# Zero matmuls in fp32, and another place for W1-W2, the transposes and the values, in a block-sorted attention with a two-way maximum layer

## The chip, the cores and the metric

The kernel runs on one core of a Trainium2 chip. The metric is the device time of one execution in microseconds (us). A core has five engines with a queue of instructions each: PE (TensorE, matmuls and transposes into PSUM; its weight loads are shown apart as PEld), DVE (VectorE), ACT (ScalarE), POOL (GpSimd, which here issues nearly all loads) and SP (SyncE, which issues the stores). An engine takes its instructions in the order of the program and stops at one whose operands are not ready. Line numbers are those of the kernel before (L77), unless a row is said to be of the changed kernel, whose lines lie a few numbers further on.

## What is computed

For 4 batches of 8 heads, 768 positions and 64 values per head, an 8 x 8 matrix `P` per head is normalised five times along rows and columns. With it the 8 blocks of 96 positions of `k` and `v` are mixed. Each block of `q` then attends to its mixed block alone. The result, 3072 tokens of 512 values, goes through a layer that takes the larger of two products.

```python
for _ in range(5):
    P = np.exp(P - np.max(P, axis=-1, keepdims=True))
    P = P / (np.sum(P, axis=-1, keepdims=True) + 1e-09)
    P = P / (np.sum(P, axis=-2, keepdims=True) + 1e-09)
k_sorted = np.einsum('bhij,bhjcd->bhicd', P, k_b)
v_sorted = np.einsum('bhij,bhjcd->bhicd', P, v_b)
scores = scale * np.matmul(q_b, k_sb.transpose(0, 1, 2, 4, 3))
attn = np.exp(scores - np.max(scores, axis=-1, keepdims=True))
attn = attn / (np.sum(attn, axis=-1, keepdims=True) + 1e-09)
x = np.matmul(attn, v_sb)          # then 3072 tokens x 512
g = np.maximum(x @ w1, x @ w2)
out = g @ w_out                    # 3072 x 512
```

## The kernel before

The maximum is rewritten: max(x W1, x W2) = relu(x (W1-W2)) + x W2. So the kernel makes W1-W2 in place of W1 (`w_difference(t)`, a quarter of the columns each, on DVE, L456), the product Wc = W2 W_out (`w2_transposes` on PE, L424, copied to `w2T`; `w_product`, L445), and then out = relu(x (W1-W2)) W_out + x Wc. A unit `moe_h(b, ch, t)` (L472) makes two of the eight 128-row blocks of the hidden layer for half a batch's tokens, 8 matmuls of 384 columns; it needs the whole of xT for that half, and quarter t of W1-W2. Its relu goes to ACT (L482) or DVE (L484) into `g`. A unit `moe_out` (L500, L508) makes 128 tokens of the output.

Attention of a batch is in eight parts u. `scores(b, u)` (L345, 8 matmuls) is followed by the exponential on ACT (L353, `e`); `values(b, u)` (L370, 8 matmuls) by a reciprocal and a product on DVE (L381, L383, `x`); `x_transposes(b, t)` (L400) turns the x of parts 2t and 2t+1 and a copy on ACT or DVE puts them into xT. Parts 0 to 3 (transposes 0 and 1) belong to the first half of the batch's tokens, units h 0 to 3; the others to units h 4 to 7. In this text scores 3, values 4, W1-W2 2 and so on have these numbers, from 0.

Ahead of the attention, k and v of two batches are mixed by block-diagonal matrices: `block_diagonals` makes them from P (L230 and four steps on DVE), `sort_v(0, t)` (L322) and `sort_k(0, t)` (L305) apply them, eight and six times. sort_k takes 64 small matmuls per two t, and each two t use one third of k_raw, which is loaded in three chunks. The second half, batches 2 and 3, is prepared later in the same way, and its `block_diagonals(1)`, L230, is the first work on PE after unit h 7 of batch 0.

The order on each engine is written out by hand (`manual_schedule`): the calls in the kernel's body are the order. Before the loop over batches they are listed one by one. In the loop a batch is a list of `units`, and `tail[n]` holds what stands right behind unit n. Only the engine of some copies is found by a rule (`pick`, with a running load of ACT and DVE). PSUM is a pool of four buffers used in turn: the fifth user of the pool waits until what the first wrote is read.

`keep_streaming(ps, n)` issues n matmuls with an all-zero tile `fill` into a buffer that is written afterwards anyway. Their result is used nowhere. They stand ahead of L230 (33), sort_v 0 (16), sort_k 2 and 4 (3 and 4), scores 0 (3) and values 0 (2).

POOL issues the loads in this order: v (6), q of batch 0, k (6), the columns of W2 and W1 in turn (8), W_out (2), q of batch 1, then v and k of the second half (`load_rest`) and the last two q. All loads convert fp32 to bf16.

Of the kernel before, what the change touches and what calls it, by code (L numbers as in the profile page):

```python
# [10 lines left out]
FP32 = mybir.dt.float32  # L11
BF16 = mybir.dt.bfloat16
# [3 lines left out]
def kernel(  # L16
# [17 lines left out]
    nc = tc.nc  # L34
# [4 lines left out]
    B, H, S, D = q.shape  # L39
# [11 lines left out]
    TCH = S // 2  # L51
# [3 lines left out]
    const = ctx.enter_context(tc.tile_pool(name="const", bufs=1))  # L55
# [12 lines left out]
    def ps_bf16(name):  # L68
        return psum.tile([128, 2048], BF16, tag="ps", name=name)

    fill = const.tile([128, 512], BF16, tag="fill", name="fill")
    nc.vector.memset(fill, 0.0)  # L72

    def keep_streaming(ps, n):

        for _ in range(n):
            nc.tensor.matmul(ps[:, 0:512], fill[:, 0:128], fill, start=True, stop=True)  # L77


    load = {"A": 0.0, "D": 0.0}  # L80
# [237 lines left out]
    def sort_v(sb, t, n=0):  # L318
        ps = ps_f32("v_ps")
        keep_streaming(ps, n)  # L320
        for d in range(8):
            nc.tensor.matmul(  # L322
                ps[:, d * 128 : (d + 1) * 128],
                v_dc[:, (t * 8 + d) * BLK : (t * 8 + d) * BLK + 128],
                bd_v[sb],
                start=True,
                stop=True,
            )
# [60 lines left out]
        load["D"] += 900  # L389
        x_tiles[b, u] = x  # L390

    def x_transposes(b, t):

        ih, hh = divmod(t, 2)
        ps = ps_bf16("tx_ps")
        for n in range(2):
            x = x_tiles.pop((b, t * 2 + n))
            for ii in range(4):
                m = n * 4 + ii
                nc.tensor.matmul(  # L400
                    ps[:, m * BLK : (m + 1) * BLK],
                    x[:, ii].rearrange("p t d -> p (t d)"),
                    ident[0:BLK, 0:BLK],
                    is_transpose=True,
                    start=True,
                    stop=True,
                )
        evac(
            xT[:, b, ih, hh * 2 : hh * 2 + 2, :].rearrange(
                "p h (i c r) -> p (h i) c r", r=R, c=PB  # L410
            ),
            ps[:, 0 : 2 * TCH].rearrange("p (m r c) -> p m c r", r=R, c=PB),
            2 * TCH,
        )
# [5 lines left out]
    def w2_transposes(t):  # L420
        ps = ps_bf16("tw_ps")
        for n in range(16):
            fb, dmt = t * 4 + n // 4, n % 4
            nc.tensor.matmul(  # L424
                ps[:, n * 128 : (n + 1) * 128],
                w2_sb[:, dmt, fb * 128 : (fb + 1) * 128],
                ident,
                is_transpose=True,
                start=True,
                stop=True,  # L430
            )
        evac(
            w2T[:, t * 4 : t * 4 + 4, :].rearrange("p f d -> p (f d)"),
            ps,
            2048,
            two_x=True,
            eng="D",
        )

    def w_product(t):  # L440
# [23 lines left out]

    g_tiles = {}

    def moe_h(b, ch, t):
        ps = ps_f32("h_ps")
        for m in range(2):
            fb = t * 2 + m  # L470
            for hp in range(HP):
                nc.tensor.matmul(  # L472
                    ps[:, m * 512 : m * 512 + TCH],
                    w1_sb[:, hp, fb * 128 : (fb + 1) * 128],
                    xT[:, b, ch, hp, :],
                    start=(hp == 0),
                    stop=(hp == HP - 1),
                )
        g = gpool.tile([128, 2, TCH], BF16, tag="g", name="g")
        src = ps.rearrange("p (t f) -> p t f", t=2)[:, :, 0:TCH]  # L480
        if pick((200 + 2 * TCH) / 1.2, (130 + 2 * TCH) / 0.96) == "A":
# [59 lines left out]
    sinkhorn(4)  # L541
    turn_v("A", 8, 24)
    turn_v("D", 24, 32)
    block_diagonals(0, 33)
    turn_v("A", 32, 46)
    turn_v("D", 46, 64)
    turn_v("D", 64, 84)
    turn_v("A", 84, 96)
    for t in range(8):
        sort_v(0, t, 16 if t == 0 else 0)  # L550
        if t in (3, 5):
            q_transposes(0, (t - 3) // 2)
    for t in range(6):
        sort_k(0, t, {2: 3, 4: 4}.get(t, 0))

    SC, VA, TR = att(0)
    scores(0, 0, 3)
    SC[1]()
    SC[2]()
    values(0, 0, 2)  # L560
    SC[3]()
    w_difference(0)
    VA[1]()
    SC[4]()
    VA[2]()
    SC[5]()
    TR[0]()
    VA[3]()
    SC[6]()
    w_difference(1)  # L570
    TR[1]()

    def turn(c0):
        turn_v("D", c0, c0 + 24)
# [2 lines left out]
    def load_rest():  # L577
# [3 lines left out]
        load_q(3)  # L581

    tail = {
        0: [VA[4], SC[7]],
        1: [VA[5], lambda: w_difference(2)],
        2: [VA[6], lambda: w_difference(3), TR[2]],
        3: [VA[7], lambda: w2_transposes(0), TR[3], load_rest],
        4: [lambda: w2_transposes(1)],
    }
    for b in range(B):  # L590
        units = [lambda t=t: moe_h(b, 0, t) for t in range(4)]
        units += [lambda t=t: moe_h(b, 1, t) for t in range(4)]
        if b == 0:
            units += [lambda t=t: w_product(t) for t in range(2)]
        units += [lambda ti=ti: moe_out(b, ti, b == B - 1 and ti >= 4) for ti in range(6)]
        steps, lo = [], 2
        if b < B - 1:
            steps += [lambda half=half: q_transposes(b + 1, half) for half in range(2)]
            if b == 1:
                steps += [lambda t=t: sort_k(1, t) for t in range(6)]  # L600
                steps += [lambda t=t: sort_v(1, t) for t in range(8)]
            SC, VA, TR = att(b + 1)
            steps += [SC[0], SC[1], SC[2], VA[0], SC[3], VA[1], SC[4], VA[2], SC[5], TR[0], VA[3], SC[6]]
            steps += [VA[4], TR[1], SC[7], VA[5]]
            if b == 0:
                lo = 7
                steps.insert(0, lambda: block_diagonals(1))
                steps += [lambda c=c: turn(c) for c in range(0, BLK, 24)]
        done = 0
        for n, unit in enumerate(units):  # L610
            unit()
            for step in tail.get(n, []):
                step()
            want = -(-len(steps) * max(0, n + 1 - lo) // (len(units) - 1 - lo))
            while done < min(want, len(steps)):
                steps[done]()
                done += 1
        tail = {0: [VA[6]], 1: [TR[2], VA[7]], 2: [TR[3]]}
# [28 lines left out]
```

## Time and profile before

| | before |
|---|---|
| median of 3 runs (200.22 to 202.46) | 202.43 us |
| profiled execution, its time | 202.21 us |
| its span | 200.5 us |
| PE busy | 179.9 us, 1999 matmuls; weight loads 106.2 us, 2015 |
| DVE, ACT, POOL busy | 91.4, 86.4, 27.0 us |
| zero matmuls ahead of L230 | 33 in 9.57 us |

The span runs from the first to the last instruction; 1.7 us of the execution lie outside. A row of the timeline gives start, length, engine, line, operation and operands, a count, and in brackets how long the engine was idle before it and what ended that. "issue" there is an idle time for which the profile shows no reason. Matmuls overlap, so a group's length is a little more than the distance to the next one; the chain of waits shows that distance.

### The profile page before, as it was taken

How to read it: one execution, taken by the hardware profiler on the slowest of the kernel's cores; microseconds unless marked ns; L12 is line 12 of the kernel's file. 1: busy time of each engine (PE TensorE's matmuls, PEld its weight loads, DVE VectorE, ACT ScalarE, POOL GpSimd, SP SyncE). 2: the span in 40 equal slices, each digit the busy share in tenths (PEclk: the TensorE clock that was granted, in tenths of full speed). 3: DMA queues.
4: the chain of work that ended last, by engine and by line, in shares of the span. 5: the costliest groups of instructions: out<-in, count | busy, mean ns of one | idle time of the engine just before them, and what ended most of it. 6: DMA issues, size and time to landing. Idle time of an engine off the chain costs nothing.

```text
span 200.5 us, 4485 instructions
## 1 busy us (share of the span) xinstructions
PE 179.9 (90%) x1999; PEld 106.2 (53%) x2015; DVE 91.4 (46%) x173; ACT 86.4 (43%) x102; POOL 27.0 (13%) x47
## 2 busy tenths in 40 slices
PE   7979759595789999899999999999999999999991
PEld 2437545353556445545867645446665555664440
DVE  4887624823533053669237615625483232630200
ACT  3296645630446613303897742415843332431020
POOL 7653554313401000000000000000000000000000
PEclk9999996966999999999999999999999999999999
DMA  3999999999997900212100002022000211200232
GB/s 47 154 202 213 202 197 197 206 209 210 209 208 121 158 2 0 108 74 88 51 3 3 0 3 105 22 86 105 3 0 3 105 53 52 108 2 0 105 128 86
DMA packets 16244, 19.19 MB, mean 96 GB/s; under 512 B 2400, under 2 KB 11616, under 8 KB 16224
## 3 DMA queue, kind: packets, MB, share of 16 engines
q0 software_dynamic: 12896, 12.59, 38.3%
q1 hardware_dynamic: 3328, 6.30, 8.4%
q8 instruction: 16, 0.26, 0.5%
q14 instruction: 4, 0.03, 0.0%
HBM read 25.17 MB, written 6.29 MB: 157 GB/s over the span
## 4 chain that ended last, share of the span: by engine, by line
PE 71%; DMA 13%; DVE 4%; ACT 4%; issue 4%; POOL 2%; DVEq 0%; ACTq 0%; POOLq 0%
PE out_ps L500 21%; PE h_ps L472 19%; PE out_ps L508 10%; DMA v_raw<-in_v_dram 7%; DMA q_raw<-in_q_dram 6%; PE wc_ps L445 4%; PE k_ps L305 3%; PE o_ps L370 3%; PE v_ps L322 3%; PE s_ps L345 3%; PE tq_ps L281 2%; PE tx_ps L400 2%; POOL v_raw L129 2%; DVE o L96 1%; ACT qT L94 1%
## 5 line engine op out<-in xcount | busy, mean ns | idle before, releaser
L472 PE MATMUL h_ps<-xT,w_sb 128*128 128x384 bf16 x256 | 48.7, 338 | 4.6 <-DVE w_sb L456 3.5
L500 PE MATMUL out_ps<-wo_sb,g 128*128 128x512 bf16 x182 | 44.5, 379 | 2.4 <-DVE o L96 0.9
L353 ACT ACTIVATE e<-s_ps 96x768 bf16<-96x768 f32 x32 | 24.6, 808 | 26.2 <-PE s_ps L345 26.2
L472 PEld LDWEIGHTS <-w_sb 128*128 128x128 bf16 x256 | 24.1, 100 | 20.9 <-DVE w_sb L456 3.7
L500 PEld LDWEIGHTS <-g 128*128 128x128 bf16 x192 | 17.9, 97 | 21.0 <-issue 1.9
L482 ACT ACTIVATE g<-h_ps 128x768 bf16<-128x768 f32 x20 | 16.3, 814 | 25.3 <-PE h_ps L472 25.3
L508 PE MATMUL out_ps<-wc,xT 128*128 128x512 bf16 x96 | 24.6, 379 | 0.0
L383 DVE TENSOR_TENSOR x<-o_ps,rs 96x512 bf16<-96x512 f32 x32 | 22.0, 686 | 1.1
L94 ACT COPY o<-out_ps 128x1024 f32<-128x1024 f32 x7 | 7.1, 1013 | 32.0 <-PE out_ps L508 27.5
L381 DVE RECIPROCAL rs<-o_ps 96x8 f32<-96x8 f32 x32 | 6.4, 199 | 28.9 <-PE o_ps L370 28.9
L484 DVE TENSOR_SCALAR g<-h_ps 128x768 bf16<-128x768 f32 x12 | 11.5, 958 | 16.5 <-PE h_ps L472 16.5
L508 PEld LDWEIGHTS <-xT 128*128 128x128 bf16 x96 | 9.4, 98 | 11.3
L370 PEld LDWEIGHTS <-e 96*128 96x128 bf16 x256 | 11.9, 100 | 4.3 <-issue 0.7
L370 PE MATMUL o_ps<-v_sb,e 96*128 96x65 bf16 x256 | 13.9, 197 | 0.0
L94 ACT CAST v_sb<-v_ps 96x1024 bf16<-96x1024 f32 x11 | 10.7, 1022 | 3.9 <-PE v_ps L322 3.9
L77 PEld LDWEIGHTS <-fill 128*128 128x128 bf16 x61 | 6.1, 108 | 10.4 <-issue 4.4
L305 PE MATMUL k_ps<-bk,k_raw 64*64 64x64 bf16 x384 | 7.9, 195 | 3.6 <-issue 3.4
L96 DVE COPY xT<-tx_ps 128x768 bf16<-128x768 bf16 x8 | 7.6, 953 | 7.7 <-PE tx_ps L400 7.7
L96 DVE CAST kT<-k_ps 128x1024 bf16<-128x1024 f32 x5 | 6.1, 1225 | 10.9 <-PE k_ps L305 10.8
L345 PE MATMUL s_ps<-qT,kT 64*128 64x96 bf16 x256 | 10.6, 213 | 0.2
L77 PE MATMUL pe<-fill 128*128 128x512 bf16 x33 | 9.6, 462 | 1.3 <-DVE fill L72 1.3
L96 DVE COPY o<-out_ps 128x1024 f32<-128x1024 f32 x4 | 4.9, 1225 | 12.1 <-PE out_ps L508 12.1
(65 smaller groups left out, 171.6 us busy)
## 6 DMA issues: line engine op xcount, KB each, us to landing
out_dram<-o SPq DMA_DIRECT2D x11, 512.0 KB, 2.8
v_raw<-in_v_dram POOLq DMA_DIRECT2D x12, 256.0 KB, 11.7
q_raw<-in_q_dram POOLq DMA_DIRECT2D x4, 768.0 KB, 12.1
k_raw<-in_k_dram POOLq DMA_DIRECT2D x12, 256.0 KB, 12.5
w_sb<-in_moe_w_dram POOLq DMA_DIRECT2D x8, 256.0 KB, 10.4
wo_sb<-in_moe_w_out_dram POOLq DMA_DIRECT2D x2, 512.0 KB, 12.2
out_dram<-o SPq DMA_DIRECT2D x2, 256.0 KB, 2.0
p_sb<-in_sort_net_dram SPq DMA_DIRECT2D x1, 8.0 KB, 1.6
```

Of the source, the lines that this page charges most:

```text
L77: nc.tensor.matmul(ps[:, 0:512], fill[:, 0:128], fill, start=True, stop=True)
L94: nc.scalar.copy(out=out_ap, in_=in_ap)
L96: nc.vector.tensor_copy(out=out_ap, in_=in_ap)
L305: nc.tensor.matmul(ps[r0 : r0 + 64, m * 64 : (m + 1) * 64], kv[r0 : r0 + 64, t * 16 + m, :], bd_k[sb][r0 : r0 + 64, :], start=True, stop=True,
L345: nc.tensor.matmul(ps[:, h2 * 512 + ii * BLK : h2 * 512 + (ii + 1) * BLK], kT[h2 * 64 : h2 * 64 + 64, (gp * 8 + i) * BLK : (gp * 8 + i) * ...
L353: nc.scalar.activation(out=e[:, 0 : 8 * BLK].rearrange("p (t f) -> p t f", t=2), in_=ps[0:BLK].rearrange("p (t f) -> p t f", t=2)[:, :, 0 ...
L370: nc.tensor.matmul(ps[:, h2 * 512 + ii * 65 : h2 * 512 + (ii + 1) * 65], e[:, (h2 * 4 + ii) * BLK : (h2 * 4 + ii) * BLK + 128], v_sb[:, h2 ...
L383: nc.vector.tensor_tensor(out=x.rearrange("p i t d -> p t i d"), in0=ov[:, :, :, 0:D], in1=rs.to_broadcast([BLK, 2, 4, D]), op=ALU.mult,)
L472: nc.tensor.matmul(ps[:, m * 512 : m * 512 + TCH], w1_sb[:, hp, fb * 128 : (fb + 1) * 128], xT[:, b, ch, hp, :], start=(hp == 0), stop=(hp ...
L482: nc.scalar.activation(out=g, in_=src, func=AF.Relu)
L500: nc.tensor.matmul(dst, g_tiles[b, ch, fb // 2][:, fb % 2, off : off + 128], wo_sb[:, fb, :], start=(fb == 0), stop=False,)
L508: nc.tensor.matmul(dst, xT[:, b, ch, hp, off : off + 128], wc[:, hp, :], start=False, stop=(hp == HP - 1),)
```

## The change

`fill` is fp32 in place of bf16, and `keep_streaming` takes a number of columns in place of a number of matmuls and issues one matmul per 512 columns: 8 ahead of L230 in place of 33, 4 ahead of sort_v 0 in place of 16, one of 384 and one of 512 columns in sort_k 2 and 4, one of 512 at scores 0, and one of 128 each at values 0 to 3.

W1-W2 0 moves ahead of scores 0, and 1 to 3 stand behind values 1, 3 and 5. All transposes and copies of xT for the first half, and all scores, now stand ahead of unit h 0; values 5 to 7 stand behind units h 0 to 2. Both `w2_transposes` come behind unit h 3, around transposes 3, and the second one's copy goes to ACT. In batch 0 the relu of units h 0 to 3 and the copies of transposes 0 and 1 are set to ACT.

```diff
-    fill = const.tile([128, 512], BF16, tag="fill", name="fill")
+    fill = const.tile([128, 512], FP32, tag="fill", name="fill")
...
-        for _ in range(n):
-            nc.tensor.matmul(ps[:, 0:512], fill[:, 0:128], fill, start=True, stop=True)
+        while n > 0:
+            w = min(n, 512)
+            nc.tensor.matmul(ps[:, 0:w], fill[:, 0:128], fill[:, 0:w], start=True, stop=True)
+            n -= w
...
-    block_diagonals(0, 33)
+    block_diagonals(0, 8 * 512)
...
-        sort_v(0, t, 16 if t == 0 else 0)
+        sort_v(0, t, 4 * 512 if t == 0 else 0)
...
-        sort_k(0, t, {2: 3, 4: 4}.get(t, 0))
+        sort_k(0, t, {2: 384, 4: 512}.get(t, 0))
 
     SC, VA, TR = att(0)
-    scores(0, 0, 3)
+    w_difference(0)
+    scores(0, 0, 512)
     SC[1]()
     SC[2]()
-    values(0, 0, 2)
+    values(0, 0, 128)
     SC[3]()
-    w_difference(0)
-    VA[1]()
+    values(0, 1, 128)
+    w_difference(1)
     SC[4]()
-    VA[2]()
+    values(0, 2, 128)
+    x_transposes(0, 0, "A")
+    values(0, 3, 128)
+    w_difference(2)
     SC[5]()
-    TR[0]()
-    VA[3]()
+    VA[4]()
+    x_transposes(0, 1, "A")
     SC[6]()
-    w_difference(1)
-    TR[1]()
+    SC[7]()
...
-        0: [VA[4], SC[7]],
-        1: [VA[5], lambda: w_difference(2)],
-        2: [VA[6], lambda: w_difference(3), TR[2]],
-        3: [VA[7], lambda: w2_transposes(0), TR[3], load_rest],
-        4: [lambda: w2_transposes(1)],
+        0: [VA[5], lambda: w_difference(3)],
+        1: [VA[6], TR[2]],
+        2: [VA[7]],
+        3: [lambda: w2_transposes(0, "D"), TR[3], lambda: w2_transposes(1, "A"), load_rest],
     }
...
-        units = [lambda t=t: moe_h(b, 0, t) for t in range(4)]
+        units = [lambda t=t: moe_h(b, 0, t, None if b else "A") for t in range(4)]
```

On PE, the end of the zero matmuls ahead of L230 and the start of those of sort_v 0, before:

```order
L77 MATMUL pe<-fill 128x512
L77 LDWEIGHTS fill
L77 MATMUL pe<-fill 128x512
L230 LDWEIGHTS sel_166
L230 MATMUL pe<-p_bf,sel_166 128x64
L77 LDWEIGHTS fill
L77 MATMUL v_ps<-fill 128x512
```

and the same place in the changed kernel:

```order
L78 MATMUL pe<-fill 128x512 x8
L232 LDWEIGHTS sel_166
L232 MATMUL pe<-p_bf,sel_166 128x64
L78 MATMUL v_ps<-fill 128x512 x4
L324 LDWEIGHTS v_dc
L324 MATMUL v_ps<-bv_210,v_dc 128x128
```

In the built program an fp32 matmul has no weight load of its own row; what the chip makes of it is not told there.

On DVE, from W1-W2 1 to the x of values 6, before. The numbers at the names are those of buffers; `w1_sb` written from itself and `w2_sb` is W1-W2, `x` is the product after a values part, `g` the relu of unit h 1:

```order
L456 TENSOR_TENSOR w1_sb_84<-w1_sb_84,w2_sb_85 128x4x256
L381 RECIPROCAL rs_772<-o_ps_763 96x8
L383 TENSOR_TENSOR x_774<-o_ps_763,rs_772 96x2x4x64
L484 TENSOR_SCALAR g_795<-h_ps_786 128x768
L381 RECIPROCAL rs_806<-o_ps_797 96x8
L383 TENSOR_TENSOR x_808<-o_ps_797,rs_806 96x2x4x64
L456 TENSOR_TENSOR w1_sb_84<-w1_sb_84,w2_sb_85 128x4x256
L381 RECIPROCAL rs_831<-o_ps_822 96x8
L383 TENSOR_TENSOR x_833<-o_ps_822,rs_831 96x2x4x64
```

and in the changed kernel, from W1-W2 1 to W1-W2 3:

```order
L459 TENSOR_TENSOR w1_sb_84<-w1_sb_84,w2_sb_85 128x4x256
L383 RECIPROCAL rs_652<-o_ps_642 96x8
L385 TENSOR_TENSOR x_654<-o_ps_642,rs_652 96x2x4x64
L383 RECIPROCAL rs_676<-o_ps_666 96x8
L385 TENSOR_TENSOR x_678<-o_ps_666,rs_676 96x2x4x64
L459 TENSOR_TENSOR w1_sb_84<-w1_sb_84,w2_sb_85 128x4x256
L383 RECIPROCAL rs_700<-o_ps_691 96x8
L385 TENSOR_TENSOR x_702<-o_ps_691,rs_700 96x2x4x64
L383 RECIPROCAL rs_754<-o_ps_745 96x8
L385 TENSOR_TENSOR x_756<-o_ps_745,rs_754 96x2x4x64
L459 TENSOR_TENSOR w1_sb_84<-w1_sb_84,w2_sb_85 128x4x256
```

Before, W1-W2 2 stood behind the g of unit h 1 and the x of values 5; now it stands behind the x of values 3, W1-W2 3 behind that of values 5, and no g lies between them. From the row of L230 for the second half on, the order of every engine is the same in both kernels, but for the relu of units h 6 and 7, which DVE now takes ahead of it.

More of the change, by code (lines that the diff above doesn't have):

```diff
@@ L390, in values, with x_transposes @@
         x_tiles[b, u] = x
-    def x_transposes(b, t):
+    def x_transposes(b, t, eng=None):
         ih, hh = divmod(t, 2)
@@ L413, in x_transposes @@
             2 * TCH,
+            eng=eng,
         )
@@ L418, with w2_transposes @@
     wc = big.tile([128, HP, DMODEL], BF16, tag="wc", name="wc")
-    def w2_transposes(t):
+    def w2_transposes(t, eng):
         ps = ps_bf16("tw_ps")
@@ L436, in w2_transposes @@
             two_x=True,
-            eng="D",
+            eng=eng,
         )
@@ L465, with moe_h @@
     g_tiles = {}
-    def moe_h(b, ch, t):
+    def moe_h(b, ch, t, eng=None):
         ps = ps_f32("h_ps")
@@ L480, in moe_h @@
         src = ps.rearrange("p (t f) -> p t f", t=2)[:, :, 0:TCH]
-        if pick((200 + 2 * TCH) / 1.2, (130 + 2 * TCH) / 0.96) == "A":
+        if (eng or pick((200 + 2 * TCH) / 1.2, (130 + 2 * TCH) / 0.96)) == "A":
             nc.scalar.activation(out=g, in_=src, func=AF.Relu)
```

## Prediction

> **What bounds the kernel now.** I read the page first: busy shares, granted clock, queues.
>
> ```profile
> span 200.5 us, 4485 instructions
> PE 179.9 (90%) x1999; PEld 106.2 (53%) x2015; DVE 91.4 (46%) x173; ACT 86.4 (43%) x102; POOL 27.0 (13%) x47
> ...
> PEclk9999996966999999999999999999999999999999
> ...
> q8 instruction: 16, 0.26, 0.5%
> ...
> L77 PEld LDWEIGHTS <-fill 128*128 128x128 bf16 x61 | 6.1, 108 | 10.4 <-issue 4.4
> ```
>
> PE is the bound, but the clock row dips in slices 7, 9 and 10 (30 to 50 us), so PE is not full there. The timeline of PE shows its waits in that stretch, in brackets at the end of a row:
>
> ```profile
> 21.39 1.13 PE L305 MATMUL k_ps<-bk,k_raw 64*64 64x64 bf16 x60
> 23.79 0.25 PE L305 MATMUL k_ps<-bk,k_raw 64*64 64x64 bf16 x4 [1.26 <-issue]
> ...
> 29.98 0.48 PE L305 MATMUL k_ps<-bk,k_raw 64*64 64x64 bf16 x11 [2.13 <-issue]
> ...
> 31.91 1.15 PE L345 MATMUL s_ps<-qT,kT 64*128 64x96 bf16 x24
> ...
> 38.93 0.34 PE L400 MATMUL tx_ps<-ident,x 96*128 96x96 bf16 x4 [1.35 <-DVE x L383]
> ...
> 47.18 2.74 PE L472 MATMUL h_ps<-xT,w_sb 128*128 128x384 bf16 x8 [2.23 <-DVE w_sb L456]
> ...
> 51.98 1.48 PE L472 MATMUL h_ps<-xT,w_sb 128*128 128x384 bf16 x8 [1.26 <-DVE w_sb L456]
> ...
> 55.97 1.14 PE L472 MATMUL h_ps<-xT,w_sb 128*128 128x384 bf16 x6 [0.56 <-ACT xT L94]
> ...
> 61.83 0.20 PE L230 MATMUL pe<-p_bf,sel 32*128 32x64 bf16 x1
> ```
>
> From the last row on (the mask product of the second sorting half) both kernels issue the same order, and before runs it with the clock at 9 or more throughout. So the question is when that product starts: at 61.83 now.
>
> Are the two waits on W1-W2 (w_sb) waits for data? The timeline of DVE says no for the longer one: the subtraction starts where the x ahead of it ends. The pool's rows for the last two column loads of W, issued by 26.6, give 10.4 us to landing, so all of W is there at 37.0.
>
> ```profile
> 35.42 0.20 DVE L381 RECIPROCAL rs<-o_ps 96x8 f32<-96x8 f32 x1
> ...
> 36.26 0.19 DVE L381 RECIPROCAL rs<-o_ps 96x8 f32<-96x8 f32 x1
> ...
> 45.84 0.69 DVE L383 TENSOR_TENSOR x<-o_ps,rs 96x512 bf16<-96x512 f32 x1
> 46.45 0.68 DVE L456 TENSOR_TENSOR w_sb<-w_sb 128x1024 bf16<-128x1024 bf16 x1
> ```
>
> ```profile
> L149 POOL DMA_DIRECT2D w_sb<-in_moe_w_dram x2: 742/742/742, 25.3 to 26.6; - x2
> ...
> DMA to landing us min/median/max: 10.4/10.4/10.4
> ```
>
> The subtraction waits in DVE's queue behind an x, which waits for PE: PE waits for its own earlier work.
>
> The two waits put down to "issue" stand 4+3+64+4+53 = 128 matmuls and as many weight loads apart: 256 instructions. Queue 8 moved 16 packets, and 4,014 instructions of PE over 16 are 251. I read them as PE out of instructions, a packet of 256 at a time, while the data DMAs are full.
>
> The windows of 3.41 us along the clock's steps show what waits cost besides. A row has the stretch, its length, the busy us of PE, PEld, DVE, ACT and POOL with their counts, then the granted clock, the DMA share and GB/s:
>
> ```profile
> 29.80:33.22 3.42, 2.97 (x38) 1.72 (x39) 1.22 (x1) 0.77 (x2) 1.67 (x3) 0.50 1.45 195
> ...
> 40.04:43.45 3.41, 3.29 (x24) 1.85 (x24) 0.70 (x2) 1.18 (x3) 0.87 (x2) 0.50 1.30 207
> 43.45:46.87 3.42, 1.51 (x16) 0.92 (x14) 2.29 (x5) 0.51 (x1) 0.26 (x1) 1.00 1.17 212
> 46.87:50.28 3.41, 3.10 (x18) 1.75 (x19) 0.26 (x1) 0.32 (x1) 1.42 (x4) 0.50 1.08 209
> ...
> 26.39:29.80 3.41, 1.47 (x55) 0.93 (x55) 0.82 (x1) 1.09 (x2) 2.03 (x3) 1.00 1.46 198
> ```
>
> A window in which PE was busy 1.47 or 1.51 is followed by one at half clock. Three such windows cost up to 1.7 us each. [...]
>
> **Part by part: the zero matmuls.** They keep PE busy while it waits.
>
> ```profile
> 1.26 9.57 PE L77 MATMUL pe<-fill 128*128 128x512 bf16 x33 [1.26 <-DVE fill L72]
> 11.87 0.18 PE L230 MATMUL pe<-p_bf,sel 32*128 32x64 bf16 x1 [1.03 <-DVE p_bf L203]
> 11.98 3.41 PE L77 MATMUL v_ps<-fill 128*128 128x512 bf16 x15
> 15.80 1.95 PE L322 MATMUL v_ps<-bv,v_dc 128*128 128x128 bf16 x32 [0.41 <-DVE v_dc L179]
> ```
>
> Sixteen in bf16 (a record is missing) take 3.41: 0.213 each. No row shows fp32. Call p the time of one with 512 columns: bounds are one bf16 fill (0.21) and, arbitrarily, twelve (2.6). What decides is when p starts to matter. The last chunk of k, issued at 13.5, lands 12.8 later, at 26.3, and the last third of sort_k cannot start before:
>
> ```profile
> L118 POOL DMA_DIRECT2D k_raw<-in_k_dram x1: 1032/1032/1032, 13.5 to 13.5; - x1
> ...
> DMA to landing us min/median/max: 12.8/12.8/12.8
> ```
>
> Eight fills from 1.5 on (fill's memset has twice the bytes), with the 2.5 that the cold start costs now (9.57 less 33 x 0.213), end at 4.0+8p. The product's 0.1, four more fills, 5.6 from the first sort_v to sort_k (15.80 to 21.39), 2.3 for two thirds of sort_k and 1.75p for its fills make 12.0+13.75p, which reaches 26.3 at p = 1.04. Up to there p costs nothing. A p of 0.21 would leave PE idle and cold ahead of 11.87, but then the sum stands at 14.9, 11 us ahead of the landing, which hides a slow sort_v. Past 1.04 each us of p costs 8+4+1.75 = 13.75. I take p below it, as the row nearest to it that I have is a bf16 fill and 1.04 is five of them; that is a choice.
>
> [...]
>
> What goes is instructions: 98 rows of fills ahead of sort_k become 12 (if one row each) to 48 (if each is split in four). Row 445 of PE's order (a branch, 98 of fills, 226 others, 120 of sort_k), where PE starved until 23.79, moves into the second third of sort_k, which waits for its chunk anyway. So sort_k ends at 26.3+1.1 = 27.5 instead of 30.46, kT's copy takes 1.2, and the first scores start at 28.8 instead of 31.91: **3.1 us**.
>
> ```profile
> 24.79 1.13 PE k_ps L305 x64
> ...
> 53.71 0.90 PE tw_ps L424 x16
> ...
> 84.09 0.28 PE s_ps L345 x8
> ...
> 92.51 1.30 PE h_ps L472 x8
> 93.81 0.26 PE o_ps L370 x8
> ...
> 95.37 0.34 PE tx_ps L400 x8
> ...
> 30.54 1.22 DVE L96 CAST kT<-k_ps 128x1024 bf16<-128x1024 f32 x1 [3.32 <-PE k_ps L305]
> ```
>
> **From the first scores to the mask product** before takes 61.83-31.91 = 29.9 us. PE's work there in after, by these rows of the chain at full clock (the 0.90 apart, which is also one): 8 scores of 0.28, 8 values of 0.26, 4 transposes of 0.34, 8 units h of 1.30, 2 transposes of W2 of 0.90 and 4 fills of 128 columns (0.2 each): 2.2+2.1+1.4+10.4+1.8+0.8 = **18.7**. To it come:
>
> - Instructions. The next 256 rows end in the first four scores, reached near 30. Before needed 23.79 to 29.98, 6.2 us, from one stop to the next; counted from about 24.5 that is 30.7. Between nothing and 2.7 us, I take **1.5**.
> - DVE. PSUM has four buffers, so the first unit h takes the one of values 4 (all numbered from 0), and waits until its x is made. From the end of values 1 DVE has x1, W1-W2, x2, x3, W1-W2, x4: four at 0.84 (35.42 to 36.26) and two at 0.60 (46.45 less 45.84 is 0.61): 4.6 us. PE has 3.0 in that time (four scores, three values, two transposes, two fills). **1.6** in several pieces. This is what the waits 1.35, 2.23 and 1.26 shrink to.
> - W1-W2 3 now stands on DVE behind x5 and ahead of x6 and x7. It is due near 40, after W's landing at 37.0, so it stops nothing; were it late, x6, x7 and the two PSUM buffers they hold would follow it. Columns 0 precede x0 in the same way, but were loaded first.
> - Transposes of W2 now fill the copy of xT (0.9 for 0.8), so the last 0.56 goes; g on ACT frees DVE. ACT's added copy of w2T delays g 4 and 5, whose PSUM buffers PE needs only after unit h 7. Nothing.
> - Clock. If the stop above fills half a window, one window runs at half: between nothing and 1.7, I take **1.0**.
>
> Together 18.7+1.5+1.6+1.0 = 22.8, and 28.8+22.8 = 51.6 for the product, against 61.83: 10.2 us. Its q_raw must be there:
>
> ```profile
> L106 POOL DMA_DIRECT2D q_raw<-in_q_dram x1: 886/886/886, 30.6 to 30.6; - x1
> ...
> DMA to landing us min/median/max: 15.4/15.4/15.4
> ```
>
> It lands at 46.0, and w_out ahead of it. The profiled execution took 202.21 (median of the runs 202.43): 202.2-10.2 = **192.0**.
>
> **Rivals.** *Weight loads in the open.* [...] Chance 0.12.
>
> *The starving goes on.* If instructions come 2.7 late and three windows still run at half (5.1), the gain loses 7.8-2.5 = 5.3: 197.3. For it: before had three such windows. Against it: the DVE wait of 2.23, which emptied one of them, goes. This is also how the change would not do what it says: fp32 split into so many instructions that none are saved. Chance 0.14, of which 0.04 within 2%.
>
> *Fills that do not warm.* [...] 0.08, a quarter of it worse than 206.5.
>
> *Slower.* PE itself is held by the fills in front: above p = 1.9 the whole gain is gone, above 2.2 (ten bf16 fills) it is slower by 2%, and at 2.6 it is 192.0-1.5+1.55 x 13.75 = 212. Only a row of fp32 can exclude it. 0.04.
>
> **Numbers.** The forecast keeps 0.62. 2% is what a measurement of this kernel tells from no change: below 198.4 is faster, above 206.5 slower. Faster 0.62+0.12+0.10 = 0.84, same 0.04+0.06 = 0.10, slower 0.02+0.04 = 0.06. The low end leaves out the stop and the half window (192.0-2.5 = 189.5); the high end takes in the starving rival, 197.3. Outside lie 0.04 of that rival's worse part, 0.08 and 0.04: 0.16.
>
> **What would show it.** Right: p at or below 1.05 in the fill rows; sort_k ending near 27.5; no PE wait on w_sb; mask product at 50 to 55; at most one half window after 20 us; everything behind it as long as before (138.7 us). Wrong: sort_v starting well after 16; "issue" waits above 3 us among the scores; a PE wait on x or g in the units h longer than 1 us; a second half that is longer than before.

## The result and the profile after

| | before | after |
|---|---|---|
| median of 4 runs each | 202.44 us (200.22 to 202.46) | 191.06 us (190.65 to 194.77) |
| profiled execution, its time | 202.21 us | 191.2 us |
| its span | 200.5 us | 189.5 us |
| start of the mask product of the second half | 61.83 | 50.85 |

The ratio of the times is 0.946, with a 95% interval of 0.938 to 0.954: faster by 11.4 us in the medians, by 11.0 between the two profiled executions, where 10.2 was forecast. Executions of one kernel differ by how many stretches they run at half clock (the mean clock is 0.970 in one of the four after and 0.994 to 0.998 in the others), and the ratios leave the most disturbed ones out; what lies behind that is taken up below.

The page of the changed kernel:

```profile
span 189.5 us, 4458 instructions
...
PE 177.5 (94%) x1992; PEld 105.5 (56%) x1992; DVE 90.5 (48%) x172; ACT 88.0 (46%) x103; POOL 25.8 (14%) x47
...
PEclk9999999999999999999999999999999999999998
...
q8 instruction: 15, 0.25, 0.5%
```

PE has about as much to do as before (177.5 us for 179.9), but in 11 us less. The clock row has lost its dips, and the instruction queue moved 15 packets in place of 16.

The timeline of PE, from the fills to the mask product of the second half:

```profile
1.52 9.85 PE L78 MATMUL pe<-fill 128*128 128x512 f32 x16 [1.52 <-DVE fill L72]
...
15.91 1.95 PE L324 MATMUL v_ps<-bv,v_dc 128*128 128x128 bf16 x32 [0.15 <-DVE v_dc L181]
...
24.00 1.27 PE L307 MATMUL k_ps<-bk,k_raw 64*64 64x64 bf16 x63 [0.44 <-DMA k_raw<-in_k_dram]
...
26.25 1.20 PE L307 MATMUL k_ps<-bk,k_raw 64*64 64x64 bf16 x64
...
28.89 0.50 PE L347 MATMUL s_ps<-qT,kT 64*128 64x96 bf16 x15 [0.39 <-DVE kT L98]
30.58 0.38 PE L347 MATMUL s_ps<-qT,kT 64*128 64x96 bf16 x9 [1.20 <-issue]
30.89 0.49 PE L78 MATMUL o_ps<-fill 128*128 128x128 f32 x2
31.22 0.42 PE L372 MATMUL o_ps<-v_sb,e 96*128 96x65 bf16 x8
...
35.88 0.34 PE L402 MATMUL tx_ps<-ident,x 96*128 96x96 bf16 x4 [0.46 <-DVE x L385]
...
37.11 1.46 PE L475 MATMUL h_ps<-xT,w_sb 128*128 128x384 bf16 x8 [0.44 <-ACT xT L96]
...
50.85 0.20 PE L232 MATMUL pe<-p_bf,sel 32*128 32x64 bf16 x1
```

The eight fills ahead of the product stand as 16 matmuls: the chip makes two of each. sort_k waits for its data (0.44) and no longer for instructions; its last third starts at 26.25, right behind the landing of its chunk. Of the waits in brackets before (1.35 for x, 2.23 and 1.26 for W1-W2, 0.56 for xT) only 0.46 and 0.44 are left, and no unit h waits for W1-W2. One stop of 1.20 without a reason in the profile has moved in among the scores.

The same stretch of work, from the first scores to the mask product, and what lies behind it, by windows (length, busy us of PE, PEld, DVE, ACT and POOL with counts, then clock, DMA share and GB/s), in the kernel before:

```profile
31.91:61.83 29.92, 23.48 (x259) 15.41 (x259) 13.40 (x24) 13.17 (x17) 7.54 (x13) 0.86 1.20 206
61.83:200.50 138.67, 131.02 (x1382) 76.13 (x1393) 57.39 (x87) 56.81 (x67) 0.90 (x1) 1.00 0.18 55
```

and in the changed kernel:

```profile
28.89:50.85 21.96, 19.81 (x264) 14.50 (x265) 11.29 (x22) 15.64 (x19) 7.54 (x13) 1.00 1.27 205
...
50.85:189.50 138.65, 131.88 (x1394) 76.11 (x1393) 58.27 (x88) 56.02 (x66) 2.36 (x3) 0.99 0.26 70
```

So 3.0 us were won ahead of the scores, 8.0 between them and the mask product (29.92 to 21.96), and nothing behind it (138.67 and 138.65).

### The profile page after: what moved, and what is told of

Same layout as the page of the kernel before. It is cut to its first block, busy times and chain, and to the rows that moved or that the text cites. A ratio compares the mean times of both kernels' runs of the same rounds, so it can differ in the third digit from the quotient of the medians.

```text
span 189.5 us, 4458 instructions
## 1 busy us (share of the span) xinstructions
PE 177.5 (94%) x1992; PEld 105.5 (56%) x1992; DVE 90.5 (48%) x172; ACT 88.0 (46%) x103; POOL 25.8 (14%) x47
## 4 chain that ended last, share of the span: by engine, by line
PE 75%; DMA 11%; DVE 5%; ACT 4%; issue 2%; POOL 1%; ACTq 0%; POOLq 0%
PE out_ps L503 23%; PE h_ps L475 22%; PE out_ps L511 11%; DMA k_raw<-in_k_dram 7%; PE wc_ps L448 4%; DMA v_raw<-in_v_dram 4%; PE o_ps L372 3%; PE s_ps L347 3%; PE tx_ps L402 2%; PE k_ps L307 2%; PE v_ps L324 2%; PE tq_ps L283 2%; DVE o L98 1%; ACT qT L96 1%; PE tw_ps L427 1%
## 5 line engine op out<-in xcount | busy, mean ns | idle before, releaser
L503 PE MATMUL out_ps<-wo_sb,g 128*128 128x512 bf16 x192 | 45.4, 379 | 1.6 <-DVE o L98 0.9
L475 PE MATMUL h_ps<-xT,w_sb 128*128 128x384 bf16 x256 | 45.8, 326 | 0.5 <-ACT xT L96 0.4
L485 ACT ACTIVATE g<-h_ps 128x768 bf16<-128x768 f32 x19 | 15.5, 814 | 15.0 <-PE h_ps L475 14.2
L487 DVE TENSOR_SCALAR g<-h_ps 128x768 bf16<-128x768 f32 x13 | 12.5, 958 | 19.6 <-PE h_ps L475 19.6
L347 PE MATMUL s_ps<-qT,kT 64*128 64x96 bf16 x256 | 10.0, 205 | 1.6 <-issue 1.2
L78 PE MATMUL pe<-fill 128*128 128x512 f32 x16 | 9.9, 785 | 1.5 <-DVE fill L72 1.5
L98 DVE COPY xT<-tx_ps 128x768 bf16<-128x768 bf16 x7 | 6.7, 955 | 7.7 <-PE tx_ps L402 7.7
L347 PEld LDWEIGHTS <-kT 64*128 64x128 bf16 x256 | 6.2, 94 | 7.1 <-issue 4.6
L96 ACT COPY xT<-tx_ps 128x768 bf16<-128x768 bf16 x9 | 7.2, 795 | 4.2 <-PE tx_ps L402 4.2
```

The source lines that it names most:

```text
L78: nc.tensor.matmul(ps[:, 0:w], fill[:, 0:128], fill[:, 0:w], start=True, stop=True)
L96: nc.scalar.copy(out=out_ap, in_=in_ap)
L98: nc.vector.tensor_copy(out=out_ap, in_=in_ap)
L347: nc.tensor.matmul(ps[:, h2 * 512 + ii * BLK : h2 * 512 + (ii + 1) * BLK], kT[h2 * 64 : h2 * 64 + 64, (gp * 8 + i) * BLK : (gp * 8 + i) * ...
L475: nc.tensor.matmul(ps[:, m * 512 : m * 512 + TCH], w1_sb[:, hp, fb * 128 : (fb + 1) * 128], xT[:, b, ch, hp, :], start=(hp == 0), stop=(hp ...
L487: nc.vector.tensor_scalar(out=g, in0=src, scalar1=0.0, scalar2=None, op0=ALU.max)
```

## The experiments

Medians are given with the ratio to the kernel before, measured beside it, and its 95% interval.

### The two halves of the change

**The fp32 fills alone**: the kernel before, in its old order, with

```diff
-    fill = const.tile([128, 512], BF16, tag="fill", name="fill")
+    fill = const.tile([128, 512], FP32, tag="fill", name="fill")
-    block_diagonals(0, 33)
+    block_diagonals(0, 8 * 512)
...
-    values(0, 0, 2)
+    values(0, 0, 256)
```

and the other fills as in the change.

> The kernel before with its zero matmuls in fp32 at the changed kernel's column counts (8, 4, 384 and 512 columns, 512, and 256 at values 0), and the old order of everything else. Theory: fewer instructions let sort_k end when its chunk has landed, so the first scores start at 28.9 as in the changed kernel, 3.0 earlier than before; behind them the old waits of DVE stay. The gain of 3.0 is partly lost to the stop for instructions that then falls among the scores (1.2): 199 to 200.5 us, mask product at 58.5 to 60. Rival, the order alone is worth something and PE was only early for the same waits: no change, 202, with the DVE waits longer by 3. Rival, instructions were the larger part: below 196.

199.58 us, ratio 0.988 (0.979 to 0.997). **The order alone**: the changed kernel with the bf16 fills back.

```diff
-    block_diagonals(0, 8 * 512)
+    block_diagonals(0, 33 * 512)
...
-    scores(0, 0, 512)
-    values(0, 0, 128)
+    scores(0, 0, 4 * 512)
+    values(0, 0, 512)
```

> The changed kernel with its zero matmuls back in bf16, four instructions for one of fp32 (33, 16, 3, 4, 4, and one for each of values 0 to 3). Theory: the two stops of 1.3 and 2.1 us in sort_k come back and the first scores start 2 to 3 us later (31 to 32), but the waits on x and W1-W2 stay away: 192.5 to 195 us, mask product at 52.5 to 54.5. Rival, without the fp32 fills the order gains nothing since PE is late anyway: 199 or more.

193.08 us, ratio 0.958 (0.950 to 0.965). The two ratios multiply to 0.946, the ratio of the whole change: the halves hardly touch each other. What PE waits for tells why. The waits of the fp32 fills alone, from the first scores to the mask product (waiting line, releaser, us in total, times, the longest):

```profile
PE h_ps L474 <- DVE w_sb L458: 3.2, 2, 2.2
PE tx_ps L402 <- DVE x L385: 1.5, 2, 1.4
PE h_ps L474 <- ACT xT L96: 1.1, 2, 0.6
PE s_ps L347 <- issue: 0.8, 1, 0.8
```

and with the order alone, sort_k among it:

```profile
PE k_ps L307 <- issue: 3.4, 2, 2.1
PE s_ps L347 <- DVE kT L98: 0.5, 1, 0.5
PE tx_ps L402 <- DVE x L385: 0.5, 1, 0.5
```

With the old order the waits on DVE's queue stay (3.2 and 1.5), and 1.1 on ACT's copies of xT; the two stops of sort_k go. With the new order and bf16 fills it is the other way about (3.4 in sort_k). The fills deal with instructions, the order with DVE and the copies of xT.

### Within the order: W1-W2

**W1-W2 late again**, in the changed kernel:

```diff
-    w_difference(2)
...
-        0: [VA[5], lambda: w_difference(3)],
-        1: [VA[6], TR[2]],
-        2: [VA[7]],
+        0: [VA[5]],
+        1: [VA[6], lambda: w_difference(2), TR[2]],
+        2: [VA[7], lambda: w_difference(3)],
```

> The changed kernel, but W1-W2 2 behind the x of values 6 and W1-W2 3 behind that of values 7, each right ahead of its unit h as before. Theory: unit h 2 waits for W1-W2 2 some 1.2 us and unit h 3 for 1.6, and the emptied windows of the clock cost up to 1.7 more: 194 to 196 us. Rival, the transposes' place and not that of W1-W2 made the gain: 191 to 192.

194.28 us, ratio 0.964 (0.956 to 0.971), 3.2 above the changed kernel. Its waits from the first scores to the mask product:

```profile
PE h_ps L475 <- DVE w_sb L459: 2.9, 2, 1.6
PE s_ps L347 <- issue: 1.2, 1, 1.2
PE s_ps L347 <- DVE kT L98: 0.4, 1, 0.4
PE h_ps L475 <- DVE x L385: 0.2, 1, 0.2
```

The 2.9 on W1-W2 are back, and nearly the whole loss. **W1-W2 early in the old order**: the kernel with fp32 fills alone, with

```diff
+    w_difference(0)
     scores(0, 0, 512)
...
-    w_difference(0)
     VA[1]()
+    w_difference(1)
...
     VA[3]()
+    w_difference(2)
...
-    w_difference(1)
-        0: [VA[4], SC[7]],
-        1: [VA[5], lambda: w_difference(2)],
-        2: [VA[6], lambda: w_difference(3), TR[2]],
+        0: [VA[4], lambda: w_difference(3), SC[7]],
+        1: [VA[5]],
+        2: [VA[6], TR[2]],
```

> The kernel before with fp32 fills (as in the run with these alone) and W1-W2 ahead of scores 0 and behind values 1, 3 and 4; transposes, values and copies in their old order. Theory: the two waits on W1-W2 (2.2 and 1.0) and the half windows behind them go, the waits on x (1.4) and xT (0.6 twice) stay: 195 to 197 us. Rival, W1-W2 was the whole gain of the order: 191 to 192. Rival, the waits on W1-W2 only become waits on x: 199 or more.

192.26 us, ratio 0.956 (0.950 to 0.963): 7.3 less than with the fp32 fills alone, and only 1.2 above the changed kernel. That was more than expected, but the change had done more than its lines say: with another running load, the rule for copies had put the copy of transposes 0 on ACT, where the kernel before has it on DVE (0.94 us there), and had given DVE the relu of unit h 0 in place of that of unit h 1. So the copy was put back:

```diff
-    TR[0]()
+    x_transposes(0, 0, "D")
```

> The kernel before with fp32 zero matmuls and W1-W2 moved ahead of scores 0 and behind values 1, 3 and 4 (192.26 in an earlier run), but with the copy of transposes 0 on DVE, where the kernel before has it, and not on ACT, where the rule for copies had put it in that run. Theory (the placing of W1-W2 is worth most of it, the copy's engine a part): the copy of about 0.9 us delays the x behind it, PE waits 0.5 to 1 longer, and the time is 192.8 to 193.8. Rival A (the copy's engine does not matter): 192.0 to 192.6. Rival B (the copy on ACT was the larger part of the gain): 196 or more.

195.15 us, ratio 0.968 (0.963 to 0.974), between the theory and the rival that gives the copy the larger part. It moves two things, though: the rule now has the relu of unit h 0 on ACT, and DVE has none before that of unit h 7. Waits explain little: PE waits 0.7 for an x where it waited 0.5. Most of the rest goes with the clock. In six executions of this kernel the mean clock is at most 0.986; of four of the one with the copy on ACT, three have 0.994 or more. At like clock (0.985 and 0.986, one execution each) the times are 193.21 and 194.13: 0.9 apart, the length of the copy. So of the 7.3 the placing of W1-W2 gives some 4.4 (199.58 to 195.15) with the copy left on DVE, and the copy on ACT 2.9, each with the relu that moved along; no run takes a relu by itself. Of the 2.9 about 0.9 may be the copy itself and the rest, I read, stretches at half clock that no longer come.

**The second transposes of W2**, put behind unit h 4 as before, with their copy on DVE:

```diff
-        3: [lambda: w2_transposes(0, "D"), TR[3], lambda: w2_transposes(1, "A"), load_rest],
+        3: [lambda: w2_transposes(0, "D"), TR[3], load_rest],
+        4: [lambda: w2_transposes(1, "D")],
```

> The changed kernel with the second group of W2 transposes behind unit h 4 as before, copied by DVE. Theory: unit h 4 waits 0.56 us for the copy of xT again, and nothing else: 191.4 to 192.0. Rival, the place of these transposes is worth more than the wait, 1.5 us or more (its copy or the PSUM buffers then hold units h 5 to 7): 192.5 or more.

191.64 us, ratio 0.955 (0.949 to 0.962): 0.6 above, the 0.56 for which unit h 4 then waits for xT again. The rule put some relus and copies elsewhere here too, but what lies behind the mask product takes 138.64 as in the changed kernel.

### What a fill costs, and when

**Doubled fills** in front, in sort_k and at scores 0:

```diff
-    block_diagonals(0, 8 * 512)
+    block_diagonals(0, 16 * 512)
-        sort_v(0, t, 4 * 512 if t == 0 else 0)
+        sort_v(0, t, 8 * 512 if t == 0 else 0)
-        sort_k(0, t, {2: 384, 4: 512}.get(t, 0))
+        sort_k(0, t, {2: 768, 4: 1024}.get(t, 0))
-    scores(0, 0, 512)
+    scores(0, 0, 1024)
```

> The changed kernel with twice the zero columns ahead of the product, sort_v, sort_k and the first scores (16, 8, 768, 1024 and 1024 columns or matmuls of 512), which is what a price p of 1.71 us for 512 columns would do. Theory: nothing up to p = 1.04, then 13.75 us per us: 0.67 x 13.75 = 9.2 us, less up to 1.5 of the stop for instructions: 199 to 200.5 us, first scores at 37.5 to 38.5. Rival, the fills lie wholly on the path: (1.71-0.86) x 13.75 = 11.8, 203 us. Rival, they lie wholly beside it: 191.

202.38 us, ratio 1.002 (0.998 to 1.006): as slow as before. This stands for a fill of twice the price, with twice the rows of instructions besides. So the rival in which PE is held by its own fills is real; the price, not the mechanism, kept it away. The row of its fills ahead of sort_v, with the first and the last start:

```profile
L78 PE MATMUL v_ps<-fill x16: 592/592/697, 17.6 to 24.1; 128*128 128x512 f32 x16
```

And the timeline of PE in its sort_k and at its first scores:

```profile
32.54 0.22 PE L307 MATMUL k_ps<-bk,k_raw 64*64 64x64 bf16 x3 [1.38 <-issue]
...
38.47 0.35 PE L307 MATMUL k_ps<-bk,k_raw 64*64 64x64 bf16 x11 [0.21 <-issue]
...
40.66 0.68 PE L347 MATMUL s_ps<-qT,kT 64*128 64x96 bf16 x24
```

Sixteen matmuls start in 6.5 us, 0.43 apart; two make a fill of 512 columns, so p is 0.86. I had expected the scores at 37.5 to 38.5 and the time at 199 to 200.5. They start at 40.66, since the added rows bring the stops back into sort_k (1.38 and 0.21) and kT's copy covers only part of the two fills at scores 0. No execution of it has a mean clock below 0.989. The prediction had the whole gain gone at p = 1.9; it is gone here at 2 x 0.86 = 1.7. A fill past the landing so costs more than its own length, but the stops are the work of the added rows, which a dearer fill would not have brought; this run therefore does not show at which price alone the gain is gone.

### What a fill is worth

Three kernels leave fills out of the changed one. **No fill at all**:

```diff
-    block_diagonals(0, 8 * 512)
+    block_diagonals(0, 0)
...
-    values(0, 3, 128)
+    values(0, 3, 0)
```

> The changed kernel without any zero matmul. Theory: the last chunk of k at 26 sets the end of sort_k, so the fills in front only matter through the clock and through the rows they put ahead of PE's packets. PE starts sort_v cold, some 2 us of that are hidden by the chunk; the 701st row moves behind scores 3, so the stop of 1.2 us among the scores goes: 190 to 192 us. Rival, without them the clock falls to half in several windows between 16 and 40: 193 to 197.

193.87 us, ratio 0.961 (0.955 to 0.968). **Fills in front only**, six ahead of the product and the four of sort_v:

```diff
-    block_diagonals(0, 8 * 512)
+    block_diagonals(0, 6 * 512)
-        sort_k(0, t, {2: 384, 4: 512}.get(t, 0))
+        sort_k(0, t, 0)
-    scores(0, 0, 512)
+    scores(0, 0, 0)
-    values(0, 0, 128)
+    values(0, 0, 0)
```

and so for values 1 to 3.

> The changed kernel with zero matmuls in front alone: 6 ahead of the product, 4 ahead of sort_v, none in sort_k, at the scores and at the values. Theory: PE waits for chunks of k with or without them, the clock stays full since sort_k fills over half of each window, and 40 rows fewer let the 701st row fall behind scores 2, where the stop is 0.5 us or less: 190.0 to 191. Rival, a half window or two among the scores: 192 to 194.

192.94 us, ratio 0.959 (0.954 to 0.965). **No fills at the values**, all others kept:

```diff
-    values(0, 0, 128)
+    values(0, 0, 0)
...
-    values(0, 3, 128)
+    values(0, 3, 0)
```

> The changed kernel without the four zero matmuls of 128 columns at values 0 to 3; all others stay. Theory (the attention's matmuls of 64 to 96 columns do not by themselves keep the clock up, however busy PE is recorded, and these four do): the clock falls to half for one to three windows between 30 and 41 us, the mask product of the second half starts at 52 to 54 and the time is 192 to 194. Rival (they only fill waits): the clock stays up, the wait for the first x grows by what they took, and the time is 190.5 to 191.3.

191.12 us, ratio 0.949 (0.943 to 0.955). The theory failed in the first two: I had thought that fills behind the front, where PE is recorded as busy, were not needed. Here are the windows of the kernel without fills, from the one ahead of its stop in sort_k on:

```profile
21.64:25.06 3.42, 3.42 (x123) 3.12 (x122) 2.09 (x3) 3.30 (x4) 1.93 (x3) 1.00 1.15 198
25.06:28.47 3.41, 1.23 (x78) 1.12 (x74) 1.31 (x2) 1.58 (x2) 1.61 (x3) 1.00 1.45 197
28.47:31.88 3.41, 1.98 (x75) 1.87 (x71) 2.96 (x3) 1.01 (x1) 1.84 (x4) 0.50 1.47 200
31.88:35.30 3.42, 3.16 (x58) 2.38 (x54) 1.56 (x5) 3.08 (x5) 1.65 (x3) 0.50 1.41 195
35.30:38.71 3.41, 3.40 (x57) 2.96 (x56) 3.31 (x9) 2.46 (x4) 1.09 (x2) 0.50 1.25 208
38.71:42.12 3.41, 3.28 (x27) 1.81 (x22) 0.61 (x1) 2.01 (x4) 0.54 (x1) 0.50 1.29 203
42.12:45.53 3.41, 3.41 (x42) 2.36 (x40) 2.38 (x5) 2.28 (x3) 0.54 (x1) 1.00 1.25 215
```

A stop of 2.18 us in the second row is followed by four windows at half clock, though PE is busy for 3.16 and 3.40 of the 3.41 in two of them. A busy PE alone is not what brings the clock back. The last section has what seems to.

The kernel without fills at the values has its median where the rival put it, but gave both answers at once: three executions of 190.18 to 190.44 at a mean clock of 0.996 or more, and three of 191.8 to 192.54 at 0.979 to 0.981. So I ran **the changed kernel once more**, to see how often it loses clock.

> The changed kernel itself once more, to see how often its executions lose clock windows. Of its four timed executions one lost some (194.8 at a mean clock of 0.970), three did not (190.7 to 191.2 at 0.994 and above); without the values' zero matmuls it was three of six (191.8 to 192.5 at 0.98). Theory (the small zero matmuls at the values keep the clock up): at most one or two of the six executions lie above 191.5, and the median is 190.7 to 191.3. Rival (windows are lost at random, whatever these four do): three or more lie above 191.5 and the median is 191.5 or more.

190.99 us, ratio 0.942 (0.938 to 0.946). Three of its seven executions, the profiled one among them, lie at 192.73 to 194.33 with a clock of 0.979 and less, the others at 190.86 to 190.99. With the four executions of the first result that is 4 of 11 disturbed, against 3 of 6 without the values' fills. Neither theory nor rival is decided by so few; what shows is that an undisturbed execution takes about 0.5 longer with these fills (190.65 to 191.2 against 190.18 to 190.44). The windows of its profiled execution, around its stop:

```profile
25.86:29.27 3.41, 3.05 (x82) 1.86 (x81) 2.20 (x3) 1.13 (x2) 1.83 (x3) 1.00 1.45 197
29.27:32.68 3.41, 2.34 (x47) 1.98 (x47) 1.30 (x5) 2.79 (x5) 1.86 (x3) 1.00 1.45 196
32.68:36.10 3.42, 3.42 (x44) 3.06 (x45) 2.73 (x6) 1.90 (x4) 1.50 (x3) 0.50 1.39 201
36.10:39.51 3.41, 3.28 (x35) 2.18 (x33) 1.60 (x4) 2.72 (x4) 0.70 (x2) 0.50 1.25 206
```

And of the same place in the changed kernel's first profile:

```profile
27.51:30.92 3.41, 1.83 (x27) 0.81 (x27) 1.82 (x2) 1.39 (x3) 1.70 (x3) 1.00 1.45 197
30.92:34.34 3.42, 3.42 (x66) 3.07 (x64) 2.54 (x7) 3.16 (x5) 1.73 (x3) 1.00 1.44 196
```

It is the same program. In the first profile the windows' edges happened to fall so that the stop of 1.20 shares its window with part of the fill ahead of the scores; in the second they fell 1.8 us later, the stop of 1.07 shares its window with small matmuls only, and two windows run at half.

### The stop that is left

**Fewer rows ahead of the scores**: five fills ahead of the product, none in sort_k.

```diff
-    block_diagonals(0, 8 * 512)
+    block_diagonals(0, 5 * 512)
-        sort_k(0, t, {2: 384, 4: 512}.get(t, 0))
+        sort_k(0, t, 0)
```

> The changed kernel with five zero matmuls of 512 columns ahead of the mask product in place of eight, and none in sort_k; those of sort_v, scores 0 and values 0 to 3 stay. PE then runs 20 rows fewer ahead of the scores, so the end of its second packet of 256 instructions moves from the end of scores 1 to the end of scores 2. Theory (the remaining stop of 1.2 us among the scores is PE out of instructions, and the clock stays up as long as the small zero matmuls among scores and values are there): the stop shrinks to 0.3 to 0.9, the first scores still start at 28.8, and the time is 190.2 to 190.8 against 191.1 for the changed kernel. Rival (the zero matmuls of sort_k are what keeps the clock up through the scores): the clock falls to half for at least one window between 28 and 41 us and the time is 192 to 193.

194.24 us, ratio 0.954 (0.944 to 0.963), above the theory and the rival. In the profiled execution the stop did not shrink, and three windows ran at half clock from 33.02 on, as the rival had it:

```profile
11.83 5.40 PE L78 MATMUL v_ps<-fill 128*128 128x512 f32 x8
17.06 1.95 PE L324 MATMUL v_ps<-bv,v_dc 128*128 128x128 bf16 x32
...
25.54 2.12 PE L307 MATMUL k_ps<-bk,k_raw 64*64 64x64 bf16 x101 [1.38 <-issue]
...
31.76 0.38 PE L78 MATMUL o_ps<-fill 128*128 128x128 f32 x1 [1.69 <-issue]
```

But a window from 12.54 on ran at half clock too, which neither had foreseen. The fills of sort_v took 5.40 in it (3.70 in the changed kernel), sort_v started at 17.06 and not at 15.91, and PE came later to all that follows. So this execution shows neither what fewer rows do at full clock nor that it was the fills of sort_k that were missing. One execution of the six had it (190.48 at 0.997), and it lies within the theory's range; it was not profiled.

What the run does show is the distance between the stops. From PE's restart at one to its restart at the next it is 31.76-25.54 = 6.22 us here, 29.98-23.79 = 6.19 before and 29.72-23.52 = 6.20 with the order alone. While the loads run, these kernels get 256 instructions every 6.2 us, and PE stops where it uses them up sooner. In the kernel with W1-W2 early in the old order both restarts of the new fills can be seen:

```profile
24.11 0.89 PE L307 MATMUL k_ps<-bk,k_raw 64*64 64x64 bf16 x45 [0.35 <-issue]
...
30.31 0.38 PE L347 MATMUL s_ps<-qT,kT 64*128 64x96 bf16 x9 [1.20 <-issue]
```

again 6.20 apart. That these stops are waits for instructions is not only read from their distance. The DMA records of the traces hold the instruction queue's packets, of 16,384 bytes each: the first two start at 21.45 and 27.57 before and at 21.91 and 28.24 in the changed kernel, 6.12 and 6.33 apart. These four take 0.94 to 0.97 each, and behind the two stops before (23.79 and 29.98) and the one in the changed kernel (30.58) PE goes on 1.40 to 1.44 us after one of them has landed.

In the changed kernel the first stop is hidden in the wait for data. That is why it keeps one of 1.20: row 445 is crossed 19 matmuls (0.4 us) behind the 24.00 at which the second third of sort_k gets its data, and 24.4+6.2 is 30.6, where PE restarts (30.58). I read from this that the stop is 6.2 us less what PE has to do in the 256 rows between, so that rows saved ahead of both places would not shorten it; no run shows that at full clock.

## Why the prediction was right

**The fills.** "Up to there p costs nothing": p is 0.86, below the 1.04, and sort_v starts at 15.91 (15.80 before), with no idle time for the fills to blame. That p lies below 1.04 was a choice when it was forecast, as no row then showed fp32. Both rivals on the price fall: the clock counts these matmuls (it is full from 7.03 on; without any fill, from 21.64 on), and the weight loads do not show at 512 columns. They do at 128:

```profile
L78 PEld LDWEIGHTS o_ps<-fill x8: 186/189/192, 30.9 to 33.9; 128*128 128x128 f32 x8
```

No run shows the 0.2 that the sum takes for a fill of 128 columns: the four at the values start 0.33 ahead of what follows them (30.89 to 31.22 in the timeline). A weight load of 0.19 hides behind a matmul of 0.43, and not, it seems, behind one of 0.11 (an estimate: a quarter of the 0.43, for a quarter of the columns).

**Ahead of the scores.** sort_k ends at 26.32+1.17 = 27.5 by the chain, the scores start at 28.89; the forecast was 27.5 and 28.8. The reading of the "issue" waits as packets of 256 rows carried this, and the packets' own records bear it out: row 445 went into the wait for data. The fp32 fills alone, which take nothing else away, start their scores at 28.77.

**From the scores to the product** the sum of 22.8 came out as 21.96, but its terms missed in both directions:

| term | taken | measured |
|---|---|---|
| PE's work | 18.7 | 19.8 (PE's busy time in the window) |
| instructions | 1.5 | 1.20 |
| DVE's queue | 1.6 | 0.46 (for the x of values 3) |
| ACT's copy of xT, at unit h 0 | no term | 0.44 |
| clock | 1.0 | none in this execution |

The work was too low by 1.1: 0.5 of it is the four fills, the rest, I read, what groups lose at their ends. DVE's term was too high by 1.1: PE was to wait at unit h 0 until the x of values 4 had freed its buffer, but what ended last there was ACT's copy of xT, for which the sum had no term. As the longer fills lie where PE would have waited for DVE, part of the one error may be the other. That the sum came within 0.9 of the measured time, with these errors and a clock term of 1.0 that did not come, is in part luck. The clock's term is 0 or several us by the execution, not 1.0: a run of 194.8 with a mean clock of 0.970 stands beside three of 190.7 to 191.2.

**W1-W2.** "This is what the waits 1.35, 2.23 and 1.26 shrink to": no unit h waits for W1-W2, and putting 2 and 3 back late costs 3.2. That x6 and x7 stand behind W1-W2 3 cost nothing, as said.

**Transposes of W2**: "the last 0.56 goes" and nothing else comes; undoing it costs 0.6. The two relus that DVE takes there are those of units h 5 and 7 (48.36 and 50.96), not of 6 and 7 as said ahead of the prediction.

**The step that was wrong, though it did not decide**, is the reading of the clock: "A window in which PE was busy 1.47 or 1.51 is followed by one at half clock". Windows with 2.34 (above) were followed by half clock too, and one with 1.83 was not.

**The rivals.** *The starving goes on* did not come: one stop is left, of 1.20, less than the 1.5 of the forecast's own sum, and the executions that lose clock end at 192.7 to 194.8, below its 197.3. *Slower* was at a distance: even the doubled fills only bring the old time back.

## What to carry to other kernels

Count instructions as well as time where loads fill the DMA queues: find from the stops how many rows a packet has and how long the next one takes, and use up a packet only in stretches that wait for data anyway. A preparation such as W1-W2 belongs on its engine's queue where its data has landed and ahead of operations that wait for PE; a copy on that queue may cost more than its own length where half-clock stretches come with it (2.9 here with a copy of 0.94). Judge a filler matmul by what it does for the clock in the worst position of the clock's windows, over several executions, since one profile may show the lucky one (4 of 11 executions of the changed kernel lost clock, and the first one profiled did not).

## What the runs showed of the chip that was not expected

**What the clock counts.** In these traces the clock changes in windows of 3.41 us (each of the three half stretches before the mask product in the kernel before is that long) whose edges lie at another place in each profiled execution: the first full clock begins at 7.03 in the profile after, at 5.38 in the changed kernel's second one.

Recorded busy time does not sort the windows well. A count of work does better. For each matmul, take the time that its columns need at full clock (0.213 us for 512 in bf16, by the fills before; four times that in fp32, where the doubled fills have 0.86), times its rows as a share of 128, the most that a matmul has here (64 for scores and sort_k, 96 for values and transposes of x, 128 for units h and fills). Sum it over a window (shifted by 0.15 us to the front, which fits best):

| kernel, window | recorded busy | counted work | clock of the next |
|---|---|---|---|
| after, 27.51 | 1.83 | 1.32 | full |
| after, second profile, 29.27 | 2.34 | 1.25 | half |
| same, 32.68, at half clock | 3.42 | 1.25 | half |
| same, 36.10, at half clock | 3.28 | 1.41 | full |
| no fills, 25.06 | 1.23 | 0.88 | half |
| no fills, 35.30, at half clock | 3.40 | 1.18 | half |
| no fills, 38.71, at half clock | 3.28 | 1.54 | full |
| no fills at the values, 30.04 | 2.52 | 1.15 | half |

With a bound at 1.32, fitted on the 153 windows up to 58 us of ten traces (both kernels and the first eight experiments), three come out wrong, two of them windows in which records of fills are missing from the trace. The third, 1.25 with W1-W2 late, is followed by full clock, as 1.25 above is not; and the bound is set by two windows, 1.31 ahead of a half one (before, 43.45) and the 1.32 of the table. On the same traces the best bound on recorded busy time, 1.74, leaves ten wrong, and a count without the share of rows eleven. On the 63 windows of the last four traces, which had no part in the fit, none is wrong: the largest count ahead of a half window is 1.27, the smallest ahead of a full one 1.41. So a window seems to need a count of 1.32 in its 3.41 us, some 39%, to be followed by full clock: an estimate, from these windows alone. At half clock only 1.71 can be counted in 3.41 us, and matmuls on 64 or 96 rows reach at most 0.5 or 0.75 of that, 0.85 or 1.28. That fits what the traces show: of ten that fall to half clock in this attention, eight stay there until the units h with their 128 rows begin, however busy PE is recorded (3.16 and 3.40 of 3.41 us in the kernel without fills). The other two (before at 29.80, W1-W2 late at 32.89) come back sooner, with fills on 128 rows in their half window; some of the eight have such fills too. It is a rule fitted to traces, and not one that an experiment was made for; a longer fill at scores 0, which it asks for, was not tried by itself. The doubled fills, which have 1024 columns there, agree with it: mean clock 0.989 or more in all ten executions.

**Instructions.** 6.2 us per packet of 256 rows while the loads run, from restart to restart in four kernels within 0.03 (6.19 to 6.22). With the doubled fills the restarts are 5.93 apart (32.54 and 38.47), and the second stop is one of 0.21.

**fp32** is, in these traces, two matmuls (16 rows for the eight fills) with a weight load each of 0.19 us (about 0.10 for bf16 in the same profile); four rows of the packet for one instruction of the program. Counted so, the first stop in sort_k stands within one row of the same place in all six kernels that have one, with none, 9, 13 or 24 fp32 fills ahead of it, or with 49 in bf16.
